# Gated linear attention and a maxout feed-forward: from one head at a time to all heads per chunk, with both stages interleaved

## The chip, the cores and the metric

The kernel runs on one core of a Trainium2 chip, in one launch. The metric is the time of one execution on the device in microseconds (us). The kernel before takes 413.72 us (median of 3 runs, 413.2 to 414.59). Engines: TensorE (PE; its weight loads are listed as PEld), VectorE (DVE), ScalarE (ACT), GpSimd (POOL), SyncE (SP), and 16 DMA engines that serve the queues of SP and ACT.

## The reference, cut to what matters

```python
# q, k, v, alpha: (4, 8, 768, 48) float32, alpha in 0.8 .. 1.0
state = np.zeros((B, H, D, D))
for t in range(S):
    state = alpha[:, :, t, :, None] * state + np.einsum('bhd,bhe->bhde', k[:, :, t], v[:, :, t])
    y[:, :, t] = np.einsum('bhd,bhde->bhe', q[:, :, t], state)

# x: (3072, 384), the 8 heads of a token side by side; w1, w2: (384, 1024); w_out: (1024, 384)
x = y.transpose(0, 2, 1, 3).reshape(B * S, H * D)
out = np.maximum(x @ w1, x @ w2) @ w_out
```

## The kernel before, in words

The recurrence is computed in chunks of 128 tokens. With a running sum of log alpha inside the chunk, the outputs of a chunk are a masked product of scaled q and scaled k with v, plus scaled q times the state that the chunk begins with; the state is then scaled and a product of scaled k with v is added.

The first stage is `gla_head`, called for each of 4 x 8 (batch, head) pairs. It loads the head's four tensors (768 x 48 each, as 128 partitions of 6 chunks; q and alpha on SP's queue, k and v on ACT's), takes the logarithm of alpha (line 86), makes one product for the sums that k needs (91) and its exponential (93), casts q, k and v, and scales k (102). Then come two groups of three chunks. Per group there are sums in transposed layout (114) and their exponentials with either sign (122, 123, 126). Per chunk: two transposes to PSUM (131, 132), a VectorE multiplication by the exponentials (134), the score product over 48 partitions (136), the mask (138), a scaled q (140), two products into the output (141, 142), and the state's product (143) and update (145). A group's output goes to SBUF (154) and, per head, by DMA into `xT`, which holds x transposed (160 to 172). 32 heads x 6 chunks are 192 passes through that body. Logarithm and exponential alternate on ScalarE, each time with a table load.

The second stage begins when the first's PSUM is given back (179). For each of 6 windows of 512 tokens it makes, for each of 8 slices of 128 of the hidden width, three matmuls for h1 (194) and three for h2 (196), copies h1 out of PSUM (198) and takes the maximum with h2 (199). Then, per 128 tokens, eight matmuls with w_out (204), a copy (209) and a store (210).

The order of instructions on each engine is chosen by the framework's planner from the order of the program; a semaphore stands at each dependence.

## Time and profile before

| | |
|---|---|
| time, median of 3 runs | 413.72 us |
| profiled execution: span from first to last instruction | 412.1 us (no other time of it is given) |
| busy, share of the span | PE 83%, DVE 61%, ACT 49%, PEld 44%, POOL 11% |
| instructions | 5,933, of these 1,856 matmuls |
| DMA | 31.05 MB, 107,855 packets, most of them under 512 B |

The profile is one execution. Busy times are sums over the instructions of an engine, and a matmul's time is from its start to its modelled end, so that matmuls which follow each other overlap. Idle time before an instruction is put down to what released it last.

### The profile page before, as it was taken

What the parts mean: (1) busy time and instruction counts of PE and PEld (TensorE: products, weight loads), DVE (VectorE), ACT (ScalarE), POOL (GpSimd) and SP (SyncE); (2) the same over time, 40 slices, a digit from 0 to 9 for tenths busy, and PEclk for the clock granted to TensorE, in tenths of its full rate; (3) what the DMA queues carried; (4) which work ended last, traced back from release to release, by engine and by line L of the source; (5) the groups of instructions that cost most, each with busy time, mean ns of one, the idle gap of its engine ahead of it and who ended that gap; (6) DMA issues with size and microseconds to landing.
All of it is one profiled execution on the core that took longest, in us unless ns stands there. A gap on an engine that the chain in (4) does not pass through costs nothing. (4 is left out here: it accounts for less than half of the span.)

```text
span 412.1 us, 5933 instructions
## 1 busy us (share of the span) xinstructions
PE 343.6 (83%) x1856; PEld 181.5 (44%) x1856; DVE 250.9 (61%) x977; ACT 202.9 (49%) x390; POOL 45.9 (11%) x82
## 2 busy tenths in 40 slices
PE   0036888888888888888888888888898999999996
PEld 0013444444444444444444444444443545545543
DVE  0134777777777777777777777777884342442441
ACT  0148656556556556656556656656201344344342
POOL 4330111112111111111111111111100000000000
PEclk9999999999999999999999999999999999999999
DMA  7992253333443333443333444211000012012012
GB/s 291 280 173 43 59 105 69 67 64 67 90 97 75 64 66 65 85 99 77 66 64 64 86 96 81 51 36 37 10 13 9 21 58 76 19 59 76 21 59 76
DMA packets 107855, 31.05 MB, mean 75 GB/s; under 512 B 101424, under 2 KB 107056, under 8 KB 107824
## 3 DMA queue, kind: packets, MB, share of 16 engines
q1 hardware_dynamic: 54192, 16.52, 18.1%
q10 hardware_dynamic: 53632, 14.16, 15.5%
q8 instruction: 14, 0.23, 0.2%
q14 instruction: 17, 0.14, 0.1%
HBM read 23.59 MB, written 4.72 MB: 69 GB/s over the span
## 5 line engine op out<-in xcount | busy, mean ns | idle before, releaser
L131 PE MATMUL qkT<-ident,q 128*48 128x128 f16 x192 | 57.7, 301 | 23.7 <-DVE q L99 23.7
L138 DVE TENSOR_TENSOR PTm<-pp,u 128x128 f16<-128x128 f32 x192 | 54.8, 286 | 31.2 <-PE pp L136 22.6
L199 DVE TENSOR_TENSOR gT<-h1s,h2p 128x512 f16<-128x512 f16 x48 | 33.0, 688 | 58.1 <-ACT h1s L198 30.2
L122 ACT ACT_TABLE_LOAD x30 | 38.5, 1283 | 48.8 <-DVE QKs L134 47.6
L122 ACT ACTIVATE AAm<-csA 48x396 f16<-48x396 f32 x64 | 31.6, 494 | 59.5 <-DVE QKs L134 58.8
L132 PE MATMUL qkT<-ident,k 128*48 128x128 f16 x192 | 60.3, 314 | 0.0
L143 PE MATMUL aux<-vh,KL 128*48 128x48 f16 x192 | 45.6, 238 | 16.0 <-POOL KL L102 12.4
L141 PE MATMUL yt<-PTm,vh 128*48 128x128 f16 x192 | 52.4, 273 | 7.1 <-DVE PTm L138 5.6
L134 DVE TENSOR_TENSOR QKs<-qkT,AAm 48x256 f16<-48x256 f16 x192 | 52.9, 276 | 6.4 <-ACT AAm L123 1.9
L136 PE MATMUL pp<-QKs 48*128 48x128 f16 x192 | 54.7, 285 | 0.0
L86 ACT ACT_TABLE_LOAD x31 | 39.8, 1283 | 19.1 <-POOL vh L101 18.6
L198 ACT CAST h1s<-h1p 128x512 f16<-128x512 f32 x48 | 28.1, 586 | 42.1 <-PE h1p L194 42.1
L114 PE MATMUL csA<-mrec,loga 128*48 128x132 f16 x192 | 34.2, 305 | 17.2 <-ACT ALE L126 13.8
L142 PE MATMUL yt<-QA,S16n 48*48 48x128 f16 x160 | 47.8, 299 | 0.0
L143 PEld LDWEIGHTS <-KL 128*48 128x48 f16 x192 | 28.2, 147 | 42.4 <-POOL KL L102 24.1
L140 DVE TENSOR_SCALAR QA<-QKs,ALE 48x128 f16<-48x128 f16 x192 | 46.2, 241 | 0.0
L145 DVE SCALAR_TENSOR_TENSOR S16n<-S16n,ALE,aux 48x48 f16<-48x48 f16 x160 | 39.7, 248 | 7.3 <-PE aux L143 7.1
L131 PEld LDWEIGHTS <-q 128*48 128x48 f16 x192 | 21.7, 113 | 45.9 <-DVE q L99 23.7
L194 PE MATMUL h1p<-xT,w 128*128 128x512 f16 x144 | 40.2, 389 | 0.6 <-DVE YTsb L154 0.6
L154 DVE CAST YTsb<-yt 48x384 f16<-48x384 f32 x64 | 35.2, 550 | 8.4 <-PE yt L142 1.6
L196 PE MATMUL h2p<-xT,w 128*128 128x512 f16 x144 | 39.7, 385 | 0.0
L101 POOL CAST vh<-vf 128x288 f16<-128x288 f32 x32 | 13.6, 424 | 234.3 <-issue 228.0
(43 smaller groups left out, 370.4 us busy)
## 6 DMA issues: line engine op xcount, KB each, us to landing
kf<-in_k_dram ACTq DMA_DIRECT2D x32, 144.0 KB, 3.3
vf<-in_v_dram ACTq DMA_DIRECT2D x32, 144.0 KB, 3.3
qf<-in_q_dram SPq DMA_DIRECT2D x32, 144.0 KB, 2.6
af<-in_alpha_dram SPq DMA_DIRECT2D x32, 144.0 KB, 3.1
out_dram<-outs ACTq DMA_DIRECT2D x24, 192.0 KB, 1.9
xT<-YTsb SPq DMA_DIRECT2D x24, 72.0 KB, 3.1
w1f<-in_moe_w_dram SPq DMA_DIRECT2D x1, 1536.0 KB, 6.8
w2f<-in_moe_w_dram SPq DMA_DIRECT2D x1, 1536.0 KB, 10.7
```

The source lines that it names most:

```text
L86: nc.scalar.activation(out=loga, in_=af, func=mybir.ActivationFunctionType.Ln)
L122: nc.scalar.activation(out=AAm[:, 0, :], in_=csA, func=mybir.ActivationFunctionType.Exp, scale=1.0)
L131: nc.tensor.transpose(qkT[:, 0, :], q16[:, c, :], ident16)
L132: nc.tensor.transpose(qkT[:, 1, :], k16[:, c, :], ident16)
L134: nc.vector.tensor_mul(out=QKs, in0=qkT, in1=AAm[:, :, jj * CW : jj * CW + C])
L136: nc.tensor.matmul(pp, lhsT=QKs[:, 1, :], rhs=QKs[:, 0, :], start=True, stop=True)
L138: nc.vector.tensor_mul(out=PTm, in0=pp, in1=u16)
L140: nc.vector.tensor_scalar(out=QA2, in0=QKs[:, 0, :], scalar1=ALE[:, jj, 1:2], scalar2=None, op0=mybir.AluOpType.mult)
L141: nc.tensor.matmul(yt[:, jj * C : (jj + 1) * C], lhsT=vh[:, c, :], rhs=PTm, start=True, stop=False)
L142: nc.tensor.matmul(yt[:, jj * C : (jj + 1) * C], lhsT=S16, rhs=QA2, start=False, stop=True)
L143: nc.tensor.matmul(pst, lhsT=KL[:, c, :], rhs=vh[:, c, :], start=True, stop=True)
L194: nc.tensor.matmul(h1p, lhsT=w116[:, ds, fsl], rhs=xT[:, ds, tkn], start=(ds == 0), stop=(ds == 2))
```

## The change

The whole body is replaced; the number formats of the products stay (fp16 in, fp32 sums). It takes the framework's manual schedule, under which each engine runs its instructions in the order in which the program writes them.

One step, called a slot, is now one chunk of 128 tokens of one batch with all 8 heads: 24 slots. The gates are summed in natural layout (tokens on partitions): one product of 384 columns gives the running sums for all heads, from which `ep` and `en` (the exponentials with either sign) scale q and k before the transposes. Heads go in pairs, padded to 64 columns each, so that one transpose serves two heads: 8 transposes per slot (`p2`), one copy out of PSUM (`v2`). The scores of the even heads use partitions 0 to 47, those of the odd heads 64 to 111 (`p3`), and land in two PSUM tiles of 512 columns, masked by one VectorE instruction each (`v3`). The state is kept per pair; its scaling is GpSimd's (`vt`). The outputs of all heads are 12 products in one PSUM tile (`p4`), copied by ScalarE (`a3`) into `xT`, whose last 32 rows per part are moved by a DMA once per three chunks.

The maximum is rewritten: max(h1, h2) = relu(h1 - h2) + h2. So `wd16` = w1 - w2 is formed once (`prep_cast`), and x @ w2 @ w_out becomes x @ m16, with m16 = w2 @ w_out computed on the chip (`prep_t`, `prep_m`). Per window of 384 tokens there are 8 steps `fstep` (three matmuls and a relu, on VectorE for three of the eight slices, else on ScalarE) and 3 steps `tstep` (3 + 8 matmuls, a copy, a store on SP's queue). They are put into three gaps of the slots: the fsteps of window w in slots 3(w+1)+1 to 3(w+1)+3, its tsteps in the last gap of the three slots after that. Slots 24 to 30 hold only such steps.

All loads are on SP's queue: three chunks, then the weights, then one chunk per slot, three slots ahead. The table set that holds logarithm and exponential is loaded once.

```diff
-    G = 3
-    NG = NCH // G
+    NCG = B * NCH
+    NP = H // 2
     NT, DM = out.shape
+    W = 384
+    CPW = W // C
+    NW = NT // W
+    ctx.enter_context(tc.manual_schedule())
+    ldp = ctx.enter_context(tc.tile_pool(name="ldp", bufs=6))
+    psx = ctx.enter_context(tc.tile_pool(name="psx", bufs=3, space=bass.MemoryType.PSUM))
+    psp = ctx.enter_context(tc.tile_pool(name="psp", bufs=2, space=bass.MemoryType.PSUM))
+    psm = ctx.enter_context(tc.tile_pool(name="psm", bufs=3, space=bass.MemoryType.PSUM))
+    nc.scalar.preload_act_table_set("natural_log_exp_and_others")
+    def load(n):
+        b, c = divmod(n, NCH)
+        got = []
+        for src, tag in ((alpha, "af"), (q, "qf"), (k, "kf"), (v, "vf")):
+            t = ldp.tile([128, H, D], FP32, tag=tag, name=tag)
+            nc.sync.dma_start(
+                out=t, in_=src[b, :, c * C : (c + 1) * C, :].rearrange("h p d -> p h d")
+            )
+            got.append(t)
+        loads[n] = got
+    for n in range(3):
+        load(n)
...
-    w1f = wtp.tile([128, 3, DFF], FP32)
-    w2f = wtp.tile([128, 3, DFF], FP32)
-    wof = wtp.tile([128, 8, DM], FP32)
-    nc.sync.dma_start(out=w1f, in_=moe_w1.rearrange("(s p) f -> p s f", p=128))
-    nc.sync.dma_start(out=w2f, in_=moe_w2.rearrange("(s p) f -> p s f", p=128))
-    nc.sync.dma_start(out=wof, in_=moe_w_out.rearrange("(s p) d -> p s d", p=128))
-    nc.gpsimd.tensor_copy(out=w116, in_=w1f)
-    nc.gpsimd.tensor_copy(out=w216, in_=w2f)
-    nc.gpsimd.tensor_copy(out=wo16, in_=wof)
...
-    def gla_head(b, h):
-        nc.sync.dma_start(out=qf, in_=q[b, h].rearrange("(c p) d -> p c d", p=128))
-        nc.scalar.dma_start(out=kf, in_=k[b, h].rearrange("(c p) d -> p c d", p=128))
-        nc.scalar.dma_start(out=vf, in_=v[b, h].rearrange("(c p) d -> p c d", p=128))
-        nc.sync.dma_start(out=af, in_=alpha[b, h].rearrange("(c p) d -> p c d", p=128))
...
+    logas = [constp.tile([128, H, 64], FP16, name=f"loga{i}") for i in range(NB)]
+    qts = [constp.tile([128, H, 64], FP16, name=f"qt{i}") for i in range(2)]
+    kts = [constp.tile([128, H, 64], FP16, name=f"kt{i}") for i in range(2)]
+    v16s = [constp.tile([128, NP, 144], FP16, name=f"v16_{i}") for i in range(NB)]
+    T16s = [constp.tile([128, NP, 96], FP16, name=f"T16_{i}") for i in range(2)]
...
+    w1f = constp.tile([128, 3, DFF], FP32)
+    wd16 = constp.tile([128, 3, DFF], FP16)
+    w2T = constp.tile([128, NF, DM], FP16)
+    m16 = constp.tile([128, 3, DM], FP16)
+    def load_weights():
+        for src, t in ((moe_w2, w2f), (moe_w1, w1f)):
+            nc.sync.dma_start(out=t[0:96], in_=src[0:288].rearrange("(s p) f -> p s f", p=96))
+            nc.sync.dma_start(out=t[96:128], in_=src[288:384].rearrange("(s p) f -> p s f", p=32))
+        nc.sync.dma_start(out=wof, in_=moe_w_out.rearrange("(s p) d -> p s d", p=128))
+    load_weights()
...
+    def a1(n):
+        af = loads[n][0]
+        nc.scalar.activation(out=logas[n % NB][:, :, 0:D], in_=af, func=ACTF.Ln)
+    def p1(n):
+        loga = logas[n % NB]
+        cs = psx.tile([128, H * D + 2 * NP], FP32, tag="x", name="cs")
+        nc.tensor.matmul(cs[:, 0 : H * D], lhsT=cmat, rhs=loga[:, :, 0:D], start=True, stop=True)
+        lp = loga.rearrange("p (r t) d -> p r (t d)", t=2)
+        for r in range(NP):
+            o = H * D + 2 * r
+            nc.tensor.matmul(cs[0:112, o : o + 2], lhsT=lp[:, r, 0:112], rhs=gcol, start=True, stop=True)
...
+    def a2(n):
+        cs = st[n]["cs"]
+        csv = cs[:, 0 : H * D].rearrange("p (h d) -> p h d", h=H)
+        nc.scalar.activation(out=en, in_=csv, func=ACTF.Exp, scale=-1.0)
+        nc.scalar.activation(out=ep, in_=csv, func=ACTF.Exp)
+        nc.scalar.activation(
+            out=gg[0:112], in_=cs[0:112, H * D :].rearrange("p (r t) -> p r t", t=2), func=ACTF.Exp
+        )
...
+    def v1(n):
+        nc.vector.tensor_mul(out=qts[n % 2][:, :, 0:D], in0=qf, in1=s["ep"])
+        nc.gpsimd.tensor_mul(out=kts[n % 2][:, :, 0:D], in0=kf, in1=s["en"])
+        v16 = v16s[n % NB]
+        vfp = vf.rearrange("p (r t) d -> p r t d", t=2)
+        nc.gpsimd.tensor_copy(out=v16[:, :, 0:D], in_=vfp[:, :, 0, :])
+        nc.gpsimd.tensor_copy(out=v16[:, :, 96 : 96 + D], in_=vfp[:, :, 1, :])
...
+    def vt(n):
+        if n % NCH:
+            g = wk.tile([128, NP], FP32, tag="g")
+            nc.gpsimd.tensor_mul(out=g[0:112], in0=st[n - 1]["gg"][0:112, :, 1], in1=s["gg"][0:112, :, 0])
+            gb = g[0:112].unsqueeze(2).to_broadcast([112, NP, D])
+            w = st[n - 1]["w"]
+            T16 = T16s[n % 2]
+            nc.gpsimd.tensor_mul(out=T16[0:48, :, 0:D], in0=w[0:48], in1=gb[0:48])
+            nc.gpsimd.tensor_mul(out=T16[64:112, :, D : 2 * D], in0=w[64:112], in1=gb[64:112])
+            if n % NCH < NCH - 1:
+                t32 = wk.tile([128, NP, D], FP32, tag="t32")
+                nc.gpsimd.tensor_mul(out=t32[0:112], in0=w[0:112], in1=gb)
+                s["t32"] = t32
...
+    def p2(n):
+        tp = psx.tile([128, 2 * NP, 128], FP16, tag="x", name="tp")
+        qp = qts[n % 2].rearrange("p (r t) d -> p r (t d)", t=2)
+        kp = kts[n % 2].rearrange("p (r t) d -> p r (t d)", t=2)
+        for r in range(NP):
+            nc.tensor.transpose(tp[:, r, :], qp[:, r, :], ident16)
+        for r in range(NP):
+            nc.tensor.transpose(tp[:, NP + r, :], kp[:, r, :], ident16)
...
+    def v2(n):
+        qk = wk.tile([128, 2 * NP, 128], FP16, tag="qk")
+        nc.vector.tensor_copy(out=qk, in_=st[n]["tp"])
...
+    def p3(n):
+        qk = st[n]["qk"]
+        pa = psp.tile([128, NP, 128], FP32, tag="p", name="pa")
+        pb = psp.tile([128, NP, 128], FP32, tag="p", name="pb")
+        for r in range(NP):
+            for o, ps in ((0, pa), (64, pb)):
                 nc.tensor.matmul(
+                    ps[:, r, :], lhsT=qk[o : o + D, NP + r, :], rhs=qk[o : o + D, r, :], start=True, stop=True
                 )
+        if n % NCH < NCH - 1:
+            kv = psx.tile([128, NP, D], FP32, tag="x", name="kv")
+            kt, v16 = kts[n % 2], v16s[n % NB]
+            for r in range(NP):
+                for t in range(2):
+                    nc.tensor.matmul(
+                        kv[64 * t : 64 * t + 64, r, :],
+                        lhsT=kt[:, 2 * r + t, :],
+                        rhs=v16[:, r, 96 * t : 96 * t + D],
+                        start=True,
+                        stop=True,
+                    )
...
+    def v3(n):
+        s = st[n]
+        pt = wk.tile([128, 2, NP, 128], FP16, tag="pt")
+        ub = u16.unsqueeze(1).to_broadcast([128, NP, 128])
+        for t in range(2):
+            nc.vector.tensor_mul(out=pt[:, t], in0=s["pp"][t], in1=ub)
+        c = n % NCH
+        if c < NCH - 1:
+            w = wk.tile([128, NP, D], FP32, tag="w")
+            if c == 0:
+                nc.vector.tensor_copy(out=w[0:112], in_=s["kv"][0:112])
+            else:
+                nc.vector.tensor_add(out=w[0:112], in0=s["kv"][0:112], in1=s["t32"][0:112])
...
+    def p4(n):
+        s = st[n]
+        y = psm.tile([128, NP, 128], FP32, tag="m", name="y")
+        v16 = v16s[n % NB]
+        for r in range(NP):
+            if n % NCH:
+                nc.tensor.matmul(
+                    y[0:96, r, :], lhsT=T16s[n % 2][0:112, r, :], rhs=s["qk"][0:112, r, :], start=True, stop=False
                 )
+            for t in range(2):
+                nc.tensor.matmul(
+                    y[0:96, r, :],
+                    lhsT=v16[:, r, 48 * t : 48 * t + 96],
+                    rhs=s["pt"][:, t, r, :],
+                    start=(n % NCH == 0 and t == 0),
+                    stop=(t == 1),
+                )
+        s["y"] = y
...
+    def a3(n):
+        nc.scalar.copy(out=xT[0:96, :, n * C : (n + 1) * C], in_=st[n]["y"][0:96])
+        if n % CPW == CPW - 1:
+            w = n // CPW
+            for i in range(3):
+                nc.scalar.dma_start(
+                    out=xT[96:128, i, w * W : (w + 1) * W], in_=xT[32 * i : 32 * i + 32, 3, w * W : (w + 1) * W]
+                )
...
+    def prep_cast():
+        nc.gpsimd.tensor_copy(out=w216, in_=w2f)
+        nc.vector.tensor_sub(out=wd16, in0=w1f, in1=w2f)
+        nc.gpsimd.tensor_copy(out=wo16, in_=wof)
+    def prep_t(f):
+        tp = psx.tile([128, 2 * NP, 128], FP16, tag="x", name="wtp")
+        for i in range(2):
+            for s in range(3):
+                nc.tensor.transpose(tp[:, 3 * i + s, :], w216[:, s, (f + i) * 128 : (f + i + 1) * 128], ident16)
+        nc.vector.tensor_copy(out=w2T[:, f : f + 2, :].rearrange("p i m -> p (i m)"),
+                              in_=tp[:, 0:6, :].rearrange("p i m -> p (i m)"))
+    def prep_m(s):
+        mp = psm.tile([128, DM], FP32, tag="m", name="mp")
+        for f in range(NF):
+            nc.tensor.matmul(mp, lhsT=w2T[:, f, s * 128 : (s + 1) * 128], rhs=wo16[:, f, :],
+                             start=(f == 0), stop=(f == NF - 1))
+        nc.scalar.copy(out=m16[:, s, :], in_=mp)
...
+    def fstep(w, f):
+        if f == 0:
+            gts[w] = mo.tile([128, NF, W], FP16, tag="g16", name="g16")
+        h = psm.tile([128, W], FP32, tag="m", name="h")
+        for s in range(3):
+            nc.tensor.matmul(h, lhsT=wd16[:, s, f * 128 : (f + 1) * 128], rhs=xT[:, s, w * W : (w + 1) * W],
+                             start=(s == 0), stop=(s == 2))
+        if f in (2, 4, 7):
+            nc.vector.tensor_relu(gts[w][:, f, :], h)
         else:
+            nc.scalar.activation(out=gts[w][:, f, :], in_=h, func=ACTF.Relu)
+    def tstep(w, i):
+        t0 = w * W + i * 128
+        op = psm.tile([128, DM], FP32, tag="m", name="op")
+        for s in range(3):
+            nc.tensor.matmul(op, lhsT=xT[:, s, t0 : t0 + 128], rhs=m16[:, s, :], start=(s == 0), stop=False)
+        for f in range(NF):
+            nc.tensor.matmul(op, lhsT=gts[w][:, f, i * 128 : (i + 1) * 128], rhs=wo16[:, f, :],
+                             start=False, stop=(f == NF - 1))
+        os_ = mo.tile([128, DM], FP32, tag="outs", name="outs", bufs=3)
+        nc.scalar.copy(out=os_, in_=op)
+        nc.sync.dma_start(out=out[t0 : t0 + 128, :], in_=os_)
...
+    LAG = 1
     for w in range(NW):
+        s0 = CPW * (w + 1) + LAG
+            put(s0 + f // 3, f % 3, fstep, w, f)
+        for i in range(3):
+            put(s0 + 3 + i, 2, tstep, w, i)
+    put(2, 0, prep_cast)
+    for f in range(0, NF, 2):
+        put(2 + f // 4, 1 + (f // 2) % 2, prep_t, f)
+    for s in range(3):
+        put(4, s, prep_m, s)
...
+    a1(0)
+    p1(0)
+    a1(1)
+    a2(0)
+    v1(0)
+    p1(1)
+    for n in range(max(NCG, last + 1)):
+        if n < NCG:
+            if n + 3 < NCG:
+                load(n + 3)
+            p2(n)
+            v2(n)
+            a2(n + 1)
+            gap(n, 0)
+            a1(n + 2)
+            p3(n)
+            v1(n + 1)
+            v3(n)
+            vt(n + 1)
+            gap(n, 1)
+            p1(n + 2)
+            p4(n)
+            a3(n)
+            gap(n, 2)
+        else:
+            for i in range(3):
+                gap(n, i)
```

## Rows read from the trace of the kernel before

**Rows 1.** The page, part 1: busy us, share of the span, instructions of each engine.

```profile
PE 343.6 (83%) x1856; PEld 181.5 (44%) x1856; DVE 250.9 (61%) x977; ACT 202.9 (49%) x390; POOL 45.9 (11%) x82
```

**Rows 2.** Two stretches: length, busy us (count) by engine, granted clock, DMA share, GB/s.

```profile
100.00:150.00 50.00, 43.55 (x242) 23.57 (x242) 37.69 (x163) 28.86 (x56) 6.68 (x12) 1.00 0.38 78
320.00:400.00 80.00, 80.00 (x412) 40.17 (x411) 28.62 (x42) 33.99 (x62) 0.00 (x0) 1.00 0.13 50
```

**Rows 3.** The chain of waits in order of time: start us, length us, what.

```profile
313.06 1.44 PE h1p L194 x3
314.50 1.28 PE h2p L196 x3
...
317.80 0.65 PE h1p L194 x3
...
325.57 5.20 PE outp L204 x32
...
403.37 5.21 PE outp L204 x32
```

**Rows 4.** TensorE in order of time, 152.9 to 154.5 us: start us, length us, instruction.

```profile
153.31 0.28 PE L136 MATMUL pp<-QKs 48*128 48x128 f16 x1
153.52 0.30 PE L131 MATMUL qkT<-ident,q 128*48 128x128 f16 x1
153.62 0.31 PE L132 MATMUL qkT<-ident,k 128*48 128x128 f16 x1
```

**Rows 5.** Groups by line: output<-inputs, shapes, count | busy us, mean ns | idle before.

```profile
L138 DVE TENSOR_TENSOR PTm<-pp,u 128x128 f16<-128x128 f32 x192 | 54.8, 286 | 31.2 <-PE pp L136 22.6
L134 DVE TENSOR_TENSOR QKs<-qkT,AAm 48x256 f16<-48x256 f16 x192 | 52.9, 276 | 6.4 <-ACT AAm L123 1.9
...
L154 DVE CAST YTsb<-yt 48x384 f16<-48x384 f32 x64 | 35.2, 550 | 8.4 <-PE yt L142 1.6
L199 DVE TENSOR_TENSOR gT<-h1s,h2p 128x512 f16<-128x512 f16 x48 | 33.0, 688 | 58.1 <-ACT h1s L198 30.2 <-PE h2p L196 27.9
...
L143 PEld LDWEIGHTS <-KL 128*48 128x48 f16 x192 | 28.2, 147 | 42.4 <-POOL KL L102 24.1 <-issue 18.0
L198 ACT CAST h1s<-h1p 128x512 f16<-128x512 f32 x48 | 28.1, 586 | 42.1 <-PE h1p L194 42.1
...
L102 POOL TENSOR_TENSOR KL<-kf,Rt 128x288 f16<-128x288 f32 x32 | 23.4, 730 | 19.3 <-ACT ALE L126 7.3 <-issue 7.3 <-ACT Rt L93 4.7
...
L204 PEld LDWEIGHTS <-gT 128*128 128x128 f16 x192 | 18.8, 98 | 13.1
...
L86 ACT ACTIVATE loga<-af 128x288 f16<-128x288 f32 x32 | 14.2, 443 | 6.0 <-DMA af<-in_alpha_dram 5.7
L101 POOL CAST vh<-vf 128x288 f16<-128x288 f32 x32 | 13.6, 424 | 234.3 <-issue 228.0 <-DMA vf<-in_v_dram 6.4
...
L209 ACT COPY outs<-outp 128x384 f32<-128x384 f32 x24 | 11.5, 480 | 22.9 <-PE outp L204 22.9
```

**Rows 6.** All engines in order of time, 20.5 to 24 us: start us, length us, instruction.

```profile
20.76 2.75 POOL L67 CAST wo<-wof 128x3072 f16<-128x3072 f32 x1
...
22.37 1.30 DVE L99 CAST q<-qf 128x288 f16<-128x288 f32 x1 [6.66 <-DMA qf<-in_q_dram]
...
23.73 0.30 PE L131 MATMUL qkT<-ident,q 128*48 128x128 f16 x1 [23.73 <-DVE q L99]
```

**Rows 7.** Two stretches, columns as in rows 2: small pieces; rows of weights.

```profile
24.00:28.00 4.00, 1.32 (x9) 0.70 (x7) 0.62 (x2) 2.39 (x4) 0.00 (x0) 1.00 1.44 187
6.00:7.00 1.00, 0.00 (x0) 0.00 (x0) 0.00 (x0) 0.00 (x0) 0.00 (x0) 1.00 1.03 398
```

**Rows 8.** DMA queues and issues, 24 to 28 us; then line 80's landing times.

```profile
q1 hardware_dynamic: 3979, 0.75, 144.2%
...
qf<-in_q_dram SPq DMA_DIRECT2D x3, 144.0 KB, 4.0
...
DMA to landing us min/median/max: 2.3/2.6/7.9
```

More of the change, by code (lines that the diff above doesn't have):

```diff
@@ L6 @@
 from concourse import bass_utils, mybir
-from concourse.masks import make_identity, make_upper_triangular, make_lower_triangular
+from concourse.masks import make_identity, make_upper_triangular
 from concourse._compat import with_exitstack
@@ L175 @@
[L175 to L185 removed]
+    half1 = constp.tile([128, 128], FP16)
+    nc.gpsimd.memset(half1, 0.0)
+    nc.gpsimd.memset(half1[0:64, :], 1.0)
+    cmat = constp.tile([128, 128], FP16)
+    nc.vector.tensor_sub(out=cmat, in0=u16, in1=half1)
@@ L200 @@
-        for tk in range(4):
-            t0 = w * 512 + tk * 128
-            outp = moeps.tile([128, DM], FP32, tag="outp", bufs=2)
-            for f in range(NF):
-                nc.tensor.matmul(
-                    outp, lhsT=gT[:, f, tk * 128 : (tk + 1) * 128], rhs=wo16[:, f, :],
-                    start=(f == 0), stop=(f == NF - 1),
-                )
-            outs = moep.tile([128, DM], FP32, tag="outs", bufs=3)
-            nc.scalar.copy(out=outs, in_=outp)
-            nc.scalar.dma_start(out=out[t0 : t0 + 128, :], in_=outs)
+            put(s0 + f // 3, f % 3, fstep, w, f)
@@ new lines, with gap @@
+        for i in range(3):
[5 more added lines that the diff above has]
+        put(4, s, prep_m, s)
+    def gap(slot, i):
+        for fn, args in gaps.get((slot, i), ()):
+            fn(*args)
+    a1(0)
[4 more added lines that the diff above has]
+    p1(1)
+    last = max(s for s, _ in gaps)
+    for n in range(max(NCG, last + 1)):
[19 more added lines that the diff above has]
+                gap(n, i)
```

173 lines of the change are left out of this document (51 added, 122 removed).

## The prediction

> **What bounds the kernel now.** I read the page's busy shares first, then the stretches, then the chain of waits in order of time, then the groups by line. TensorE is busy for 343.6 of 412.1 us [rows 1], but this is an average over two stages that have different limits [rows 2]. From 320 to 400 us TensorE is busy in every microsecond, and the chain of waits there is nothing but matmuls: three of 512 columns take 0.65 us, that is 0.216 us each, and 32 of 384 columns take 5.20 us, 0.1625 us each [rows 3]. The maxout stage is bound by columns streamed: per 512 tokens 48 x 0.216 + 32 x 0.1625 = 15.6 us, six times 93.4 us.
>
> The attention stage fills the rest. A matmul of 128 columns takes about 0.29 us from start to end, but starts come 0.10 us apart where nothing intervenes, and 0.21 us apart where a product over 48 partitions is followed by a transpose over 128 [rows 4]. So the "busy" 43.55 of 50 us [rows 2] is mostly pipeline depth. The stage runs from its first matmul at 23.73 us [rows 6] to 313.06 us: 289 / 192 = 1.51 us for one head and one chunk, 12 us for eight heads. It is a ping-pong of small steps: TensorE waits for VectorE and VectorE for TensorE, with 192 calls each of lines 134 and 138 alone [rows 5].
>
> The clock needs care. The granted clock reads 1.00 in both stretches [rows 2], yet the first triples of 512 columns at 313 us take 1.28 to 1.44 us and those from 317.80 us take 0.65 [rows 3]: 512 columns in 0.43 us is the 1.2 GHz level, in 0.216 us the 2.4 GHz level. The 0.10 us for 128 columns in the attention stage is also the lower level (128 / 1.2 = 107 ns). So the attention stage ran at 1.2 GHz throughout, and the clock rose only after some 4 us of dense matmuls.
>
> **The change, part by part.** One slot is now one chunk of 128 tokens for all eight heads, 24 slots, and TensorE's order in a slot is fixed: p2 (8 transposes), a maxout step, p3 (8 score products, 8 key-value products), a maxout step, p1 (one of 384 columns, four tiny ones), p4 (12 products), in two slots of three a maxout step, then an output step.
>
> The maxout work is the plainest term. h1 and h2 become one product with the weight difference (3 matmuls of 384 columns per step, 0.49 us), and the second term goes through a precomputed 384 x 384 matrix (11 matmuls of 384 columns per output step, 1.79 us) [rows 3]. 64 x 0.49 + 24 x 1.79 = 74 us against 93, at the upper clock.
>
> For a small matmul at 2.4 GHz there is no row. By columns it is 128/384 of 0.1625 = 0.054 us; the rows at the lower clock give 0.107. Weights that are narrower than 128 columns loaded in 0.147 us on average (line 143) against 0.098 for 128 wide (line 204) [rows 5], and many here are 48 to 112 wide; so I take 0.09, nearer the upper end.
>
> The other engines, per slot: VectorE copies 1,024 fp16 columns of transposes out of PSUM. Line 134 does 256 fp16 columns in 0.276, line 138 128 fp32 columns in 0.286, so fp16 passes two columns in the time of one: 0.155 + 1,024 x 0.00047 = 0.65 us (1.22 if at line 199's rate of 512 in 0.688). Two masks at 0.69 (line 199's shape), the q product 0.56, the state add 0.36, one relu 0.55 (line 154): 3.5 us. ScalarE: logarithm 0.52, exponentials 0.48 + 0.48 + 0.16, y 0.59 (line 198), relus 0.80, output 0.48 (line 209): 3.5 us; its table loads go. GpSimd: k product 0.92 (line 102's 0.73 scaled), v casts 0.68, state scaling 1.8: 3.4 us [rows 5]. All three fit in half a slot if the slot is over 7 us, so they matter only where TensorE waits for them.
>
> The walk through a slot at 2.4 GHz, from the start of p2: transposes end at 0.72; the last result is there 0.2 us later; the copy runs from 0.98 to 1.63. A maxout step hides it until 1.21, so TensorE waits 0.47 us. Three changes of array shape cost 0.11 each (0.21 less 0.10, rows 4). Scores 1.79 to 2.51, key-value to 3.34, maxout step to 3.94, p1 to 4.46. The masks have run from 2.86 to 4.17, so p4 doesn't wait, by 0.29 us. p4 to 5.54, 2/3 of a maxout step to 5.87, output step to 7.66 us. Bounds: 6.3 us with the 0.054 pace, 8.3 with 0.107, and 0.57 more if the copy goes at the slower rate.
>
> One cover is thin. VectorE's q product and GpSimd's k product become ready within half a microsecond of each other. A VectorE cast of 288 columns, worth 0.3 to 0.46 us by its size, took 1.30 us when it met a GpSimd cast, and ended 0.16 us after that one did [rows 6]. So the q product may be held for up to the k product's 0.9 us. In the walk I have held it until that ends, at 2.3, which costs nothing; if the v casts (0.68) go ahead of it too, the masks end at 4.85 and p4 is 0.4 us late, 7 us over 17 slots; if it is never held, nothing is gained either. The Trainium skill (SBUF — State Buffer, Who interferes with whom) says that a VectorE instruction with two SBUF inputs, as this product is, waits for a GpSimd instruction that reads SBUF. The row here shows it for a cast only; by the rule the hold is certain, without it the masks end 0.7 us sooner, and the sum is the same by both.
>
> **The start** is set by the transfers. All loads are on SP's queue: three chunks (12 transfers of 197 KB in 192-byte pieces), then 4.72 MB of weights, then chunk 3. SP's queue alone moved such pieces at 187 GB/s from 24 to 28 us, weights moved at 398 GB/s [rows 7, 8]. From 1.8 us: 12.6 us of chunks, 11.9 of weights, 1.05 for alpha of chunk 3, 1.5 for landing (2.3, the least, less its 0.8 of transfer) [rows 8]: 28.8 us. The logarithm of chunk 3 stands in slot 1 ahead of that slot's output copy on ScalarE, and p1 stands ahead of p4 on TensorE, so slot 1 stalls until about 30.9 us. Slot 2: transposes and copy to 32.7, the weight difference (3,072 columns, 3.35 us) to 36.1, q product 36.6, masks 38.0, p4 and a rest 39.4 us. GpSimd's two weight casts (2.75 each, rows 6) lie beside the stall.
>
> **The sum** on the profiled execution (span 412.1, 1.6 below the median of 413.72; no other time of it is given): 39.4; slot 3 at the lower clock, a bare chain of transposes 0.86, copy 0.65, scores 0.86, masks 1.31, p4 1.28, weight transposes 0.64 and 0.7 of handing over, 6.3; slot 4 with three weight products of 1.3 in place of the output step, 9.9; slots 5 and 6 without it, 11.7; slots 7 to 23, 17 x 7.66 = 130.2; the tail of 10 maxout and 7 output steps, 17.4; from the last matmul to the end 3.6 as now (408.6 to 412.1, rows 3). 218.5, plus 1.6: 220 us.
>
> **Rivals.** (a) The clock stays at the lower level in the mixed slots, as it did through the whole attention stage. The walk then gives 11.0 us a slot; 17 x 3.4 = 57 more, with 11 for slots 4 to 6 and the tail: 288 us. For it: in the old stage, with TensorE 87% busy by the stretch [rows 2], the clock never rose. Against: a slot at this level would have only 0.4 us of wait in 11, and the output step with the step ahead and the transposes behind is over 5 us without a gap; some 4 us raised it at 313. Swinging between levels gives 238 to 270 us. The Trainium skill (TensorE: Matmul & The Clock Gate, A second HAM failure mode: psum-queue depth-cycling) tells of a kernel whose clock swung because it cycled through PSUM banks. Lines 194 to 204 cycle through six banks and held the upper level from 317.80 us to the end, so the trace speaks against it here, but that stage had no waits.
>
> (b) Loads bound the slot. 786 KB at 187 GB/s is 4.2 us, with the output 4.7, under 7.66. At half the rate it would be 8.9 a slot, 1.2 x 20 = 25 more: 245 us. Rows 8 speak against it.
>
> (c) Slower than before: the four loads of a chunk pass SP one after the other. SP's order now also holds output stores that wait for ScalarE. At 4.0 us to landing [rows 8] for 144 KB, 4.3 for 192 KB, a chunk would need 17.2 us: 39.4 + 21 x 17.2 + 17.4 + 5 = 423 us. It turns slower from 4.2 us a transfer on. Against: five such transfers were issued from 24 to 28 us and 0.75 MB moved in those 4 us, so they overlap.
>
> **Chances.** Forecast (205 to 238 us) 0.55; swinging clock 0.18; (a) 0.12; under 205, with small matmuls near 0.054, 0.07; (b) 0.05; (c) 0.03. Under 1 in 10 lies below 198 and about 1 in 8 above 270: range 198 to 270, the forecast's own 205 to 238. Below 0.3% two times can't be told apart here; every case but (c) is far outside: faster 0.96, the same 0.01, slower 0.03.
>
> **What would show it.** Right: output steps of 1.79 us from slot 7 on, slots 7 to 8 us apart, TensorE's one regular wait the one for the copy of the transposes, the first mask of slot 2 near 37 us. Wrong: 384-column matmuls at 0.32 us between slots (a); waits for loads after 40 us (b, c); small matmuls at 0.06 or 0.11; ScalarE, VectorE or GpSimd over 70% busy in a slot, which would mean that one of their prices is off by half.

## The result, and the profile after

The changed kernel takes 212.93 us (median of 4 runs, 211.58 to 213.18) against 414.15 us for the kernel before (4 runs): a ratio of 0.514, 95% interval 0.512 to 0.515. The forecast was 220 us, its own range 205 to 238. The total came out within 4% by luck: the start took longer than forecast and the slots less, and within the slots two errors of opposite sign partly cancel as well. Most of this text is about them. Medians below are of all four executions of a run, ratios leave out one that is over 1.5% above the fastest of its run (in experiments 2 and 10, whose medians without it are 195.56 and 192.96 us).

The profiled execution took 212.77 us with a span of 211.0. First the page's head and part 1, which answer to [rows 1]:

```profile
span 211.0 us, 3834 instructions
PE 154.2 (73%) x1440; PEld 103.8 (49%) x1440; DVE 92.6 (44%) x153; ACT 76.6 (36%) x188; POOL 89.6 (42%) x168
```

VectorE has 153 instructions in place of 977, ScalarE 188 in place of 390, and no engine but TensorE is busy for half of the span. The slots are read from the first transpose of each. In profiled time:

| stretch | forecast, us | measured, us | difference |
|---|---|---|---|
| up to the start of slot 3 | 39.4 | 46.25 | +6.9 |
| slot 3 | 6.3 | 6.99 | +0.7 |
| slot 4 | 9.9 | 8.76 | -1.1 |
| slots 5 and 6 | 11.7 | 11.33 | -0.4 |
| slots 7 to 23 | 130.2 (7.66 each) | 115.6 (6.88 each up to slot 22) | -14.6 |
| tail and end, from 188.97 us | 21.0 | 22.0 | +1.0 |

**One mixed slot.** TensorE in the slot that starts at 113.31 us, in order of time (start us, length us, line and instruction; in brackets the idle time before it and what ended it). L191 are the transposes, L300 a maxout step, L207 the scores, L216 the key-value products, L247 and L251 the output's products (`p4`), L311 and L313 an output step:

```profile
113.31 0.39 PE L191 MATMUL tp<-ident,qt 128*128 128x128 f16 x4
113.53 0.39 PE L193 MATMUL tp<-ident,kt 128*128 128x128 f16 x4
113.75 0.65 PE L300 MATMUL h<-xT,wd 128*128 128x384 f16 x3
114.70 0.23 PE L207 MATMUL pa<-qk 48*128 48x128 f16 x1 [0.30 <-DVE qk L198]
114.71 0.23 PE L207 MATMUL pb<-qk 48*128 48x128 f16 x1
...
115.03 0.31 PE L216 MATMUL kv<-v,kt 128*64 128x48 f16 x8
...
116.11 0.24 PE L247 MATMUL y<-qk,T 112*96 112x128 f16 x1
116.53 0.22 PE L251 MATMUL y<-pt,v 128*96 128x128 f16 x1 [0.17 <-DVE pt L230]
117.12 0.22 PE L251 MATMUL y<-pt,v 128*96 128x128 f16 x1 [0.38 <-DVE pt L230]
...
117.69 0.65 PE L311 MATMUL op<-m,xT 128*128 128x384 f16 x3
```

Starts are what counts here. Four transposes take 0.22 us from start to start (113.31 to 113.53), 0.055 us each, which is 128 columns at 2.4 GHz. The scores start in pairs 0.01 us apart, one on partitions 0 to 47 and one on 64 to 111: eight take 0.33 us up to the key-value products, where the forecast had 0.83. The eight key-value products stream 48 columns each and take 0.24 us up to the next maxout step (115.27), where the forecast priced them like products of 128 columns, 0.72. The two waits in brackets ahead of L251 are for the masks. VectorE in the same slot:

```profile
113.96 0.69 DVE L198 COPY qk<-tp 128x1024 f16<-128x1024 f16 x1 [2.15 <-PE tp L193]
114.80 1.08 DVE L162 TENSOR_TENSOR qt<-qf,ep 128x384 f16<-128x384 f32 x1
115.80 0.68 DVE L230 TENSOR_TENSOR pt<-pa,u 128x512 f16<-128x512 f32 x1
116.40 0.68 DVE L230 TENSOR_TENSOR pt<-pb,u 128x512 f16<-128x512 f32 x1
```

The q product (L162) takes 1.08 us and stands ahead of the masks (L230). TensorE's three regular waits, over the whole span (engine and line, what it waited for, us in total, times, longest):

```profile
PE cs L135 <- ACT loga L128: 26.0, 8, 17.6
PE y L251 <- DVE pt L230: 12.3, 32, 2.2
PE pa L207 <- DVE qk L198: 8.6, 22, 0.8
```

Two thirds of the first are one wait in the start. The second, for the masks, was forecast not to be there.

**The start.** ScalarE, VectorE and GpSimd from 34 to 43 us:

```profile
34.73 0.52 ACT L128 ACTIVATE loga<-af 128x384 f16<-128x384 f32 x1 [18.12 <-DMA af<-in_alpha_dram]
...
38.93 3.80 DVE L274 TENSOR_TENSOR wd<-w1f,w2f 128x3072 f16<-128x3072 f32 x1
39.46 3.47 POOL L166 CAST v<-vf 128x192 f16<-128x192 f32 x1
```

The logarithm of chunk 3 comes at 34.73 us (28.8 was forecast), and ScalarE waited 18.12 us for it. The DMA view from 2 to 34 us tells why. The first row is the rate in 40 equal slices of 0.8 us; the others are the page's form of an issue, with KB and the median us from issue to landing:

```profile
GB/s 189 212 212 203 199 193 187 192 187 186 187 188 177 192 190 255 210 220 246 200 236 241 220 189 241 225 241 225 215 246 220 215 176 241 367 372 374 371 307 222
...
wof<-in_moe_w_out_dram SPq DMA_DIRECT2D x1, 1536.0 KB, 19.1
...
w1f<-in_moe_w_dram SPq DMA_DIRECT2D x1, 384.0 KB, 15.7
```

The chunks move at some 190 GB/s, as forecast. The second piece of w1 is issued at 13.80 and so lands at 29.5 us, w_out is issued at 14.58 and lands at 33.7. So the rate from 15 to 29 us, about 222, is that of w1 and w2, and the 370 behind it is that of w_out. In the kernel before the same bytes of w1 and w2 moved at 391 GB/s. A window of the kernel before and one of the changed kernel (length, busy us and count of PE, PEld, DVE, ACT, POOL, granted clock, DMA share, GB/s):

```profile
3.00:11.00 8.00, 0.00 (x0) 0.00 (x0) 0.00 (x0) 0.00 (x0) 2.81 (x3) 1.00 1.02 391
```

```profile
15.00:29.00 14.00, 1.96 (x26) 1.48 (x24) 3.07 (x5) 1.42 (x4) 7.42 (x11) 1.00 1.03 222
```

What stands out between them is the cut: the changed kernel loads each of the two as 96 partitions and 32 partitions, w_out as before as 128.

**Three dips.** A dip is here a stretch after the start (after 60 us) in which the granted clock of TensorE is 0.50. Three windows of 1 us, columns as just above, and below them what came before, all engines in order of time:

```profile
150.00:151.00 1.00, 0.14 (x1) 0.00 (x0) 0.37 (x1) 1.00 (x5) 0.70 (x1) 1.00 0.64 191
151.00:152.00 1.00, 0.49 (x4) 0.39 (x4) 1.00 (x2) 0.46 (x2) 1.00 (x3) 0.66 0.92 175
...
157.00:158.00 1.00, 1.00 (x10) 0.83 (x9) 0.00 (x0) 0.58 (x2) 0.00 (x0) 0.50 0.00 0
```

```profile
145.97 2.95 ACTq L265 DMA_DIRECT2D xT<-xT  x3
...
149.72 0.50 ACT L150 ACTIVATE en<-cs 128x384 f32<-128x384 f32 x1
...
150.63 1.07 DVE L162 TENSOR_TENSOR qt<-qf,ep 128x384 f16<-128x384 f32 x1 [1.86 <-ACT ep L151]
...
151.50 0.48 PE L135 MATMUL cs<-loga,cmat 128*128 128x384 f16 x1 [1.37 <-ACT loga L128]
...
151.63 0.68 DVE L230 TENSOR_TENSOR pt<-pa,u 128x512 f16<-128x512 f32 x1
```

ScalarE issues the three transfers of `xT`'s last rows, and that takes 2.95 us of its time. Its next work, an output copy (148.96 us) and the exponentials, is late. So are the logarithm, for which TensorE waits 1.37 us, the q product and the masks; TensorE is nearly idle from 150 to 151 us and about half idle up to 153. Then the granted clock is 0.50, the 1.2 GHz level, up to 158 us. It also falls to 0.50 near 73 and near 131 us, each time behind such an issue (at 67.25 and 124.67 us). Not every late slot ends so: from 89 to 90 us TensorE is idle for the same reason and the clock stays at 1.00, while ahead of 131 us it has no idle microsecond. The undisturbed slots take 6.2 to 6.7 us, two of those with a dip 8.4 and 9.7, and the late one without a dip 7.5.

### The profile page after: what moved, and what is told of

It reads as the page before. It is cut to its first block, busy times and chain, and to the rows that moved or that the text cites. A ratio compares the mean times of both kernels' runs of the same rounds, so it can differ in the third digit from the quotient of the medians.

```text
span 211.0 us, 3834 instructions
## 1 busy us (share of the span) xinstructions
PE 154.2 (73%) x1440; PEld 103.8 (49%) x1440; DVE 92.6 (44%) x153; ACT 76.6 (36%) x188; POOL 89.6 (42%) x168
## 4 chain that ended last, share of the span: by engine, by line
PE 37%; DVE 18%; SPq 15%; issue 10%; ACT 8%; ACTq 6%; DMA 4%; DVEq 0%
SPq L67 14%; PE op L313 12%; DVE pt L230 12%; PE y L251 7%; ACTq L265 6%; PE h L300 5%; PE op L311 5%; DVE qt L162 3%; DVE qk L198 3%; ACT xT L261 2%; PE mp L288 2%; DMA af<-in_alpha_dram 2%; PE y L247 2%; DMA xT<-xT 2%; ACT outs L316 2%
## 5 line engine op out<-in xcount | busy, mean ns | idle before, releaser
L163 POOL TENSOR_TENSOR kt<-kf,en 128x384 f16<-128x384 f32 x24 | 23.9, 996 | 56.6 <-ACT en L150 49.1
L300 PE MATMUL h<-xT,wd 128*128 128x384 f16 x192 | 42.0, 334 | 0.3 <-ACT outs L316 0.3
L313 PE MATMUL op<-wo,g 128*128 128x384 f16 x192 | 37.4, 341 | 0.0
L251 PE MATMUL y<-pt,v 128*96 128x128 f16 x192 | 24.8, 240 | 12.7 <-DVE pt L230 12.3
L162 DVE TENSOR_TENSOR qt<-qf,ep 128x384 f16<-128x384 f32 x24 | 23.1, 962 | 14.5 <-ACT ep L151 13.8
L313 PEld LDWEIGHTS <-g 128*128 128x128 f16 x192 | 19.6, 102 | 14.1 <-issue 2.7
L316 ACT COPY outs<-op 128x384 f32<-128x384 f32 x24 | 11.5, 479 | 40.3 <-PE op L313 23.4
L251 PEld LDWEIGHTS <-v 128*96 128x96 f16 x192 | 20.1, 140 | 8.7 <-issue 8.4
L305 ACT ACTIVATE g<-h 128x384 f16<-128x384 f32 x40 | 19.9, 500 | 8.6 <-PE h L300 6.1
L300 PEld LDWEIGHTS <-wd 128*128 128x128 f16 x192 | 16.7, 100 | 8.7 <-issue 0.9
L179 POOL TENSOR_TENSOR T<-w,g 48x192 f16<-48x192 f32 x20 | 10.0, 499 | 22.5 <-DVE w L238 16.6
L166 POOL CAST v<-vf 128x192 f16<-128x192 f32 x24 | 18.3, 761 | 0.0
L247 PE MATMUL y<-qk,T 112*96 112x128 f16 x80 | 17.4, 238 | 0.0
L230 DVE TENSOR_TENSOR pt<-pa,u 128x512 f16<-128x512 f32 x24 | 16.3, 680 | 2.2 <-PE pb L207 2.1
L207 PE MATMUL pa<-qk 48*128 48x128 f16 x96 | 10.5, 236 | 8.6 <-DVE qk L198 8.6
L311 PE MATMUL op<-m,xT 128*128 128x384 f16 x72 | 16.6, 342 | 0.0
## 6 DMA issues: line engine op xcount, KB each, us to landing
w1f<-in_moe_w_dram SPq DMA_DIRECT2D x1, 1152.0 KB, 14.6
```

Of the source, the lines that this page charges most:

```text
L162: nc.vector.tensor_mul(out=qts[n % 2][:, :, 0:D], in0=qf, in1=s["ep"])
L163: nc.gpsimd.tensor_mul(out=kts[n % 2][:, :, 0:D], in0=kf, in1=s["en"])
L166: nc.gpsimd.tensor_copy(out=v16[:, :, 0:D], in_=vfp[:, :, 0, :])
L230: nc.vector.tensor_mul(out=pt[:, t], in0=s["pp"][t], in1=ub)
L247: nc.tensor.matmul(y[0:96, r, :], lhsT=T16s[n % 2][0:112, r, :], rhs=s["qk"][0:112, r, :], start=True, stop=False)
L251: nc.tensor.matmul(y[0:96, r, :], lhsT=v16[:, r, 48 * t : 48 * t + 96], rhs=s["pt"][:, t, r, :], start=(n % NCH == 0 and t == 0), stop=(t ...
```

## The experiments

Times are medians; the kernel before took 413.8 to 413.9 us beside them. "Mixed slots" are the 16 intervals between the starts of slots 7 and 23, read from each trace: 6.88 us in the changed kernel.

**1. `xT`'s transfers on SP's queue.**

```diff
-                nc.scalar.dma_start(
+                nc.sync.dma_start(
                     out=xT[96:128, i, w * W : (w + 1) * W], in_=...
```

> The changed kernel with one edit: the three small transfers that move rows of xT are issued from SP's queue, not ACT's. Theory A: their issue (0.51 to 1.75 us each, 24 of them, 5.8% of the chain of waits) holds up ScalarE's next exponentials every third slot, those hold up the q product and the masks, and the dips of the granted clock to 0.50 follow those pauses of TensorE. Then ScalarE's queue issues nothing, the long slots (8.4 and 9.7 us) go, and the time is 201 to 208 us. Theory B: the transfers only wait elsewhere, the loads behind them on SP come later, and the dips come from the masks alone: 211 to 215 us, dips unchanged.

200.23 us (ratio 0.484, 0.482 to 0.485): 12.7 us faster. The mixed slots take 6.36 us and repeat nearly in threes (6.66, then 6.17 to 6.22, then 5.99 or 6.17), and the dips are gone in all four executions (mean granted clock 0.998 to 1.000). A window of this run, columns as above:

```profile
140.00:160.00 20.00, 17.37 (x195) 11.52 (x192) 11.75 (x20) 10.32 (x28) 11.52 (x22) 1.00 0.83 165
```

The view of waits still has TensorE's wait for the masks:

```profile
PE y L251 <- DVE pt L230: 12.8, 34, 2.4
```

So the issue of these transfers on ScalarE set off the dips, and the wait for the masks is a cost of its own. By the starts of the slots, 8.3 us were gained in slots 7 to 23 and 4.3 in slots 3 to 6.

**2. The q product behind the masks.**

```diff
     def v1(n):
-        nc.vector.tensor_mul(out=qts[n % 2][:, :, 0:D], in0=qf, in1=s["ep"])
...
             v3(n)
+            vq(n + 1)      # the q product alone
```

> The changed kernel with one edit: on VectorE the q product of the next chunk stands behind the two masks and the state add, not ahead of them. Theory A: the product (0.96 us, held by GpSimd) stands in the way of the masks, and TensorE waits 12.3 us in all for masks; with it behind them these waits go, slots 7 to 23 take 5.8 to 6.1 us in place of 6.4 to 6.7, and the time is 200 to 207 us. Theory B: the next slot's transposes then wait for the q product instead, and the wait only moves: 210 to 215 us.

195.95 us (0.472, 0.469 to 0.475): 17.0 us faster, more than either theory had. TensorE's wait for the masks and the q product's group (busy us, mean ns, idle before):

```profile
PE y L255 <- DVE pt L234: 3.7, 7, 1.8
```

```profile
L171 DVE TENSOR_TENSOR qt<-qf,ep 128x384 f16<-128x384 f32 x24 | 14.2, 591 | 5.1 <-ACT ep L151 5.0
```

The group of the changed kernel that answers to it:

```profile
L162 DVE TENSOR_TENSOR qt<-qf,ep 128x384 f16<-128x384 f32 x24 | 23.1, 962 | 14.5 <-ACT ep L151 13.8
```

The same instruction takes 962 ns beside GpSimd's k product and 591 ns away from it. But the edit changes two things at once, the order of the masks and the neighbour of the q product, and no run tells them apart. In the profiled execution (194.29 us, mean granted clock 0.999) the dips are gone too, although ScalarE still issues the transfers: a late exponential no longer delays the masks. They are not gone for good. The other three executions took 195.56 to 197.71 us at a mean granted clock of 0.980 to 0.983.

**3. Both edits.**

> Both edits: xT's transfers on SP's queue and the q product behind the masks. If each removes its own wait the gains add up: 190 to 199 us, no granted clock below 0.9 after 60 us. If they cut the same wait (ScalarE late, so q late, so masks late), the time is that of the better one, within 3 us.

190.63 us (0.461, 0.459 to 0.462). Mixed slots of 5.86 us. The gains of 12.7 and 17.0 don't add (22.3): the first edit alone removes the dips, the second a part of them. With the transfers on SP's queue already, moving the q product is worth 9.6 us (200.23 to 190.63), about what TensorE's wait for the masks loses (12.8 to 3.7). Of TensorE's waits in the mixed slots, the one for the copy of the transposes is left, as forecast:

```profile
PE pa L211 <- DVE qk L202: 8.9, 23, 0.8
PE y L255 <- DVE pt L234: 3.7, 7, 1.8
```

**4. One chunk more ahead of the weights** (in the changed kernel): `range(4)` for `range(3)`, and `load(n + 4)` in the loop.

> The changed kernel with one edit: four chunks are loaded ahead of the weights, not three (and every later load one slot earlier). Theory A: TensorE stands still from 17.7 to 35.3 us because alpha of chunk 3 is queued behind 4.7 MB of weights; with it ahead, slot 1 ends near 20 us, slot 2 stalls instead at the weight difference, which waits for the weights until about 34 us: slot 3 starts at 42 to 44 us in place of 46.25, time 208 to 211 us. Theory B: all of it waits for the weights anyway, which come 4 us later: 212 to 217 us.

208.77 us (0.504, 0.502 to 0.506), as Theory A had it. Slot 2 starts at 19.97 us in place of 37.22, then stalls itself; slot 3 starts at 42.78 in place of 46.25. What a slot does while the weights move is gained, the rest of the stall only moves by one slot.

**5. The rewriting of the maximum undone**: x @ w1 and x @ w2, a copy on ScalarE and a maximum on VectorE, no `m16`.

```diff
-        if f in (2, 4, 7):
-            nc.vector.tensor_relu(gts[w][:, f, :], h)
+        for s in range(3):
+            nc.tensor.matmul(h2, lhsT=w216[...], rhs=xT[...], ...)
+        nc.scalar.copy(out=h1s, in_=h)
+        nc.vector.tensor_max(out=gts[w][:, f, :], in0=h1s, in1=h2)
```

> The changed kernel with the rewriting of the maximum undone: per step three matmuls with w1 and three with w2, a copy of the first by ScalarE, the maximum by VectorE; no product matrix m16, no transposes of weights, 8 matmuls per output step. TensorE's columns: 64 x 0.49 more, 24 x 0.49 and about 6 us of preparation less: +14 us. Theory A: TensorE's columns are what a slot waits for, and the extra copies add waits: 225 to 235 us. Theory B: the slots are bound by the masks' chain and hide the extra columns: 211 to 217 us.

214.29 us (0.518, 0.516 to 0.519): only 0.6% more than with the rewriting, while 64 x 0.49 less 24 x 0.49 = 19.6 us of columns were added. TensorE at the place of the copy's wait:

```profile
114.40 0.23 PE L207 MATMUL pa<-qk 48*128 48x128 f16 x1
```

No idle time stands ahead of the scores: the extra products fill the 0.3 to 0.5 us for which TensorE otherwise waits for the copy. There were no dips in this run (granted clock 1.00), which hides a part of the price: its mixed slots take 7.00 us, the undisturbed ones of the changed kernel 6.5. Slot 3 begins 2.2 us earlier, since nothing is prepared.

**6. Not interleaved**: every maxout step behind slot 23.

```diff
-        s0 = CPW * (w + 1) + LAG
+        s0 = NCG + CPW * w
```

> The changed kernel without the interleaving: slots 0 to 23 hold the attention alone (and the weights' preparation), all maxout and output steps come after slot 23. Theory A: a bare slot is a chain of about 4.5 us (slots 0 and 5 took 4.5 and 4.9 us), near what the loads allow (786 KB at 187 GB/s, 4.2 us), at the lower clock; 46 + 21 x 4.8 + 74 + 8 = 229 us, so the interleaving is worth some 16 us. Theory B: without ScalarE's and VectorE's maxout work ahead of it a slot falls to the loads' 4.2 us and the dense end makes up for it: 212 to 218 us.

247.96 us (0.599, 0.596 to 0.601): interleaving is worth 35 us, and both theories missed. A window in the attention part:

```profile
80.00:120.00 40.00, 28.16 (x279) 23.00 (x277) 21.28 (x34) 13.11 (x35) 22.38 (x44) 0.50 0.80 129
```

The attention alone runs at a granted clock of 0.50. So the maxout steps do two things in a slot: they fill waits, and with them the clock stays at 2.4 GHz for the small products. What each is worth by itself wasn't measured.

**7. The scores in another order**: four of the even heads, then four of the odd heads.

```diff
-        for r in range(NP):
-            for o, ps in ((0, pa), (64, pb)):
+        for o, ps in ((0, pa), (64, pb)):
+            for r in range(NP):
```

> The changed kernel with one edit: the scores of all even heads are issued before those of all odd heads, so that two products on different rows of the array no longer follow each other. Theory A: the starts 0.01 us apart in the trace are products that run at once; in sequence they stand 0.055 us apart, eight take 0.44 us in place of 0.24. The first mask needs only the even heads, so the time hardly moves: 211 to 216 us. Theory B: the starts of the trace are drawn, not real, and nothing moves, the spacing included.

211.81 us (0.511, 0.509 to 0.514), the same time. But the trace is not what I expected of that order:

```profile
108.92 0.23 PE L207 MATMUL pa<-qk 48*128 48x128 f16 x1 [0.30 <-DVE qk L198]
108.93 0.23 PE L207 MATMUL pb<-qk 48*128 48x128 f16 x1
108.98 0.22 PE L207 MATMUL pa<-qk 48*128 48x128 f16 x1
109.00 0.22 PE L207 MATMUL pb<-qk 48*128 48x128 f16 x1
```

Products on different partitions start in pairs here too, although the program has four of one kind ahead of the first of the other. The run could not tell whether the pairing is worth anything, because the order did not take it away. Nor does it rule out Theory B, that these starts are drawn and not real. VectorE's starts in experiment 3 speak against that:

```profile
107.99 0.39 PE L195 MATMUL tp<-ident,qt 128*128 128x128 f16 x4
...
108.66 0.68 DVE L202 COPY qk<-tp 128x1024 f16<-128x1024 f16 x1
...
109.40 0.23 PE L211 MATMUL pa<-qk 48*128 48x128 f16 x1 [0.32 <-DVE qk L202]
...
109.83 0.69 DVE L234 TENSOR_TENSOR pt<-pa,u 128x512 f16<-128x512 f32 x1 [0.49 <-PE pb L211]
```

The copy starts 0.67 us behind the first of eight transposes, the mask 0.43 us behind the first score (0.65 to 0.68 and 0.43 in all the mixed slots of that trace). In the program's order the mask needs seven of the eight scores; one after the other at 0.055 us they would let it start at some 0.60 us, an estimate from the copy's 0.65.

**8. The kernel before with one table set loaded at the start**, one added line (`preload_act_table_set`).

> The kernel before with one part of the change alone: the table set that holds both logarithm and exponential is loaded once, so that up to 61 of the 62 table loads (1.28 us each) go. Theory A: ScalarE is off the path in the attention stage, TensorE and VectorE hand small steps to each other: 408 to 414 us. Theory B: the loads stand ahead of the gates' exponentials on the path of each head: 32 x 1.3 to 62 x 1.3 us less, 335 to 375 us.

396.97 us (0.958, 0.955 to 0.961): both theories missed. All of the gain lies in the attention stage, whose end the first maxout product marks, at 296.47 us:

```profile
296.47 1.44 PE h1p L195 x3
```

In the kernel before that is 313.06 [rows 3]. So 16.6 us of 78 us of table loads were on the path; the rest ran beside TensorE's work.

**9. Experiment 3 with four chunks ahead of the weights.**

> Three edits together: xT's transfers on SP's queue, the q product behind the masks, and four chunks loaded ahead of the weights. The first two gave 190.6 us, the third alone 4.2 us. Theory A: the start and the slots are separate, so 186 to 188 us. Theory B: with shorter slots TensorE waits for loads later, and nothing is gained: 189 to 192 us.

189.34 us (0.457, 0.456 to 0.459), the lowest median of this study, though its executions (188.56 to 189.78) overlap with those of experiment 3 (189.34 to 191.05). Slot 3 starts 2 us earlier than in experiment 3, and TensorE has a new wait for the cast of w2:

```profile
PE wtp L285 <- POOL w L277: 8.2, 1, 8.2
```

What the start gains is given back in slots 3 and 4: slot 7 starts at 67.05 us against 66.73, and the two profiled executions are equal (189.4 and 189.3 us). The medians differ by 1.3 us.

**10. Five chunks ahead**, the preparation and all steps one slot later (`LAG = 2`).

> As the run before, but five chunks are loaded ahead of the weights, the weights are prepared one slot later (slot 3 on), and every maxout and output step comes one slot later. Theory A: slots 0 to 2 run while the chunks land, slot 3 waits for the weights near 37 us in place of slot 2, one bare slot (4.5 to 5 us) is won and a part of it is given back at the end, where one slot's steps more stand alone: 182 to 186 us. Theory B: the weights land 4 us later and TensorE's columns are the same, so it only moves: 186 to 190 us.

193.18 us (0.465, 0.464 to 0.467): both theories missed. Slot 4 starts at 48.56 us, 0.8 earlier than in experiment 9, but slot 5, which now holds the products for `m16`, takes 11.5 us, where slot 4 with them took 9.6; and with all steps one slot later the stretch behind the start of slot 23 takes 30.3 us in place of 27.1.

**11. Experiment 3 with the rewriting undone**, as in 5.

> The kernel with both edits (xT on SP's queue, q product behind the masks; 190.6 us) and the rewriting of the maximum undone. Alone, undoing it cost 1.4 us. Theory A: that was so because each slot's waits for masks hid the 14 us of added columns, and the clock's dips were absent; with the waits gone the columns show: 200 to 206 us. Theory B: the rewriting is worth nothing in either: 190 to 194 us.

193.12 us (0.467, 0.465 to 0.468), 2.5 us above experiment 3. TensorE's waits took up a part of the 19.6 us of columns:

```profile
PE pa L211 <- DVE qk L202: 3.1, 4, 0.8
PE y L255 <- DVE pt L234: 1.8, 5, 0.4
```

That is 5.8 us less of the wait for the copy and 1.9 less for the masks than in experiment 3. Slot 3 starts 1.9 us earlier, for the preparation of `m16` falls away, which kept TensorE busy for 7.4 us in experiment 3. In the profiled executions TensorE's busy time thus rises by 12.5 us (143.4 to 155.9) and its idle time falls by 8.1; the 4.4 us that are left are the difference of the two spans (187.6 and 191.9). Mixed slots take 6.11 us, 0.25 more.

**12. Experiment 3 with the weights behind one chunk**, the weight difference and the casts in slot 0.

```diff
-    for n in range(3):
-        load(n)
+    load(0)
...
     load_weights()
+    for n in (1, 2):
+        load(n)
...
-    put(2, 0, prep_cast)
+    put(0, 0, prep_cast)
```

> As e3_both, but the weights' transfers stand behind one chunk's loads on SP's queue and not behind three, and the weight difference and the casts are put into slot 0 instead of slot 2. Theory A (the start is a matter of order on SP's queue: the weights can land and be turned into fp16 while slots 0 to 2 wait for their chunks anyway): the last weights land near 18 us in place of 30, alpha of chunk 2 near 26, slots 1 and 2 follow the loads, slot 3 starts at 35 to 38 us in place of 45.4 and the mixed slots stay at 5.5 to 6.0 us: 181 to 184 us. Theory B (all bytes have to come before chunk 3 whatever their order, and the 13 us that VectorE and GpSimd need for the weights then hold up slot 0 and 1 instead of slot 2): slot 3 starts at 42 us or later, 187 to 191 us.

193.21 us (0.466, 0.464 to 0.468): slower than experiment 3 by 2.6 us, Theory A wrong. Slot 3 starts at 49.36 us, as B had it (42 or later), but the time is above B's 187 to 191. The weights' rate is low here too. The DMA view from 2 to 26 us, in slices of 0.6 us, and the first chunk's load behind the weights:

```profile
GB/s 170 230 237 199 187 218 236 259 225 212 225 218 218 246 239 232 225 198 212 280 218 205 239 218 218 253 219 239 203 182 223 353 374 371 374 369 371 270 221 187
```

```profile
26.30 0.52 ACT L129 ACTIVATE loga<-af 128x384 f16<-128x384 f32 x1 [21.92 <-DMA af<-in_alpha_dram]
...
28.75 0.61 PE L196 MATMUL tp<-ident,qt 128*128 128x128 f16 x4 [1.12 <-DVE qt L172]
```

Alpha of chunk 1 lands near 26 us. Its logarithm stands ahead of chunk 0's exponentials in ScalarE's order, and its sums ahead of slot 0 in TensorE's, so that slot 0 starts at 28.75 us in place of 10.5. Two slots of work that had lain beside the weights' transfers came behind them. I had not counted that wait, as I had looked only at slots 1 and 2.

## Why the prediction was right, and where it was not

**What bounds the slot.** Right: TensorE's work bounds the mixed slots, the clock is at 2.4 GHz in them, the output steps take 1.79 us from 117.69 on, and the copy of the transposes is a regular wait (8.6 us in 22 waits). Experiment 3 leaves little else. Wrong by the prediction's own signs: the slots stand 6.9 us apart and not 7 to 8, the wait for the masks is larger than the one for the copy, the first mask of slot 2 starts at 43.26 us and not near 37, and small matmuls come at 0.055 us.

**The pace of small matmuls** is the first mis-sized term. I took 0.09 us, nearer the upper end of 0.054 to 0.107, because of the 0.147 us of a narrow weight load [rows 5]. It is 0.055, the lower end, for products with weights of 96 and 112 columns too (nine of them from 117.18 to 117.69 us): the loads are hidden. Added to that, the key-value products were priced by 128 columns and have 48, and the scores run two at a time, which no row of before could show. So the bound of 6.3 us that the walk gives at 0.054 is no bound: experiment 3 has 5.86. The Trainium skill (TensorE: Matmul & The Clock Gate, Part 3: Packing small matmuls) says that products on different row groups of the array run at the same time; the pairs 0.01 us apart and the early mask in experiment 3 agree with it. It also says that matmuls start in program order, and experiment 7's rows differ from that. The part of the walk from transposes to p1 falls from 4.46 to 2.80 us.

**The masks' cover** is the second, and it goes the other way. I wrote that holding the q product "costs nothing", by a slack of 0.29 us. The hold came at the size foreseen (1.08 us, ending 2.6 us after the slot's start), and the masks ended at 3.77 us, earlier than the 4.17 forecast. But TensorE was ready for p4 at 2.80 us and not at 4.46: the faster TensorE used up its own cover. This is why moving the q product gained 9.6 us where there are no dips (experiment 3 against 1), 17.0 where there are, and not nothing. The slack was computed at one end of a range whose other end reverses it.

**A price left out.** The three transfers of `xT` per window are in the change, I named SP's order, and never priced their issue on ScalarE: 24 of them at 0.51 to 1.75 us. That, with the q product and the masks behind it, made the dips. By experiment 1 it is 12.7 us. The rival "swinging clock" thus happened in three places; its 238 to 270 us was too high: 238 is 18 us over the forecast, and in the mixed slots the dips and the late slot cost about 6 (16 slots at 6.88 against 6.5 undisturbed).

**The start** is the third mis-sized term, 6.9 us of it. The weights were to take 11.9 us at 398 GB/s; they took 18.9 (from about 14.8 to 33.7 us). w1 and w2, 3.15 MB, at 222 in place of 391 GB/s are 6.1 us of that. I took the rate from transfers of 128 partitions and did not look at the cut into 96 and 32. The Trainium skill (SBUF — State Buffer, Door 1: The DMA port swizzle) says that a transfer's rate goes by the ports that its partitions reach, and that partitions 0 to 63 share half of the ports, 64 to 127 the other half. By that, 96 partitions lay two thirds of their bytes on one half, and the 32 lie on the other alone; I had not weighed it. The rows agree in direction: in experiment 12 too w1 and w2 move at some 225 and w_out, uncut, at 370. No run of the changed kernel loaded them uncut. That the cut is the cause is read from three traces and not tested by itself. The rest of the start came in the order worked out: the stall of slot 1, the weight difference in 3.80 us (3.35 forecast), the first mask of slot 2 behind it, some 6 us late. The cast of v that took 3.47 us beside it (0.76 is its mean) was not foreseen; no wait of TensorE is put down to it.

**The rivals.** (a), the lower clock all through, did not come, and experiment 6 shows how near it was: without the maxout steps in the slots the attention stays at 0.50. (b) and (c), loads: of TensorE's 26.0 us of waits for the logarithm all but 8.4 are one wait in the start, and the chunks moved at the rate taken. Under 205: its condition, the pace near 0.054, came true; the start and the masks kept the time above it, and experiments 1 to 3 reach 190 to 200 when the masks and ScalarE are freed.

**Where the two halves came from.** The interleaving is worth 35 us. The rewriting of the maximum, for which the forecast counted 19.6 us of columns, is worth 1.4 us in the changed kernel and 2.5 in experiment 3 (4.4 between the profiled executions): a part of the columns would have lain in waits, and preparing `m16` takes back another. The table loads that go were worth 17 us in the kernel before. These are about 55 of the 201 us that the change took off, a rough sum, as the three were measured in different kernels. The rest, some 145 us, stays with the attention by chunks of all heads; no run here isolates it.

## What to carry to other kernels

When you take a value inside a range, work out each "costs nothing" again at the other end: a faster bound engine shortens every cover that you drew from it. List the DMAs that an edit issues by the engine that issues them, and price the issue there as work of that engine. Before you take a transfer's rate from a row, compare the partitions of the two transfers, not only the bytes of a row.
